# Spread places for routing steps, weights issued in pieces, and part of the softmax sums moved to VectorE in an attention and mixture-of-experts kernel

## The chip, the cores and the metric

The kernel runs on one core of one Trainium2 chip. A core has five engines that run side by side, each with its own in-order queue of instructions: TensorE (PE, matrix products; its weight loads, PEld, overlap them), VectorE (DVE), ScalarE (ACT), GpSimd (POOL) and SyncE (SP, which here only issues DMAs). They meet through semaphores. The metric is the device time of the whole program in microseconds (us).

## The reference

Attention over 8 batches and 12 heads of 448 positions, with a soft cap on the scores, followed by a layer of 8 experts of which each token uses the best one, and each expert keeps at most `capacity` (80) tokens. Cut to what matters:

```python
q, k, v: (8, 12, 448, 64) float32;  cap = 30
scores = cap * tanh((q @ k.T) / 8 / cap)
scores = scores - max(scores)
attn = exp(scores);  attn = attn / (sum(attn) + 1e-9)
x = (attn @ v), heads laid side by side: (3584, 768)

logits = x @ w_gate                         # 8 experts
expert_idx = argmax(logits);  gate_w = softmax(logits)[expert_idx]
out = zeros
for e in range(8):
    tok = tokens of expert e; if more than capacity, those with the largest gate_w
    h = maximum(x[tok] @ w1[e], 0)          # (768, 1024)
    out[tok] = gate_w[tok] * (h @ w2[e])    # (1024, 768)
```

## The kernel before

**Attention.** The 96 pairs of batch and head are worked on in 24 units (`NU`) of four heads. In the loop at L1251, iteration w computes the scores and exps of unit w and, between them, the products with v, the sums and the scaling of unit w-1. The order of the work within an iteration is written out by hand in the list `STEPS` (L1249), and each engine's queue holds its instructions in that order (`manual_schedule`). The steps are:

- `q0` to `q6` (`scores`, L1028): a tile of transposed scores, keys on the partitions, in PSUM (two tiles exist), then ACT's tanh of it. A head's 448 keys are three chunks of 128 and a rest of 64. Tile 0 (L1040) holds the rests of all four heads, two heads' queries stacked on the two halves of the partitions; tiles 1 to 6 (L1049) hold the chunks.
- `e0` to `e3` (`expo`, L1052): ACT's exps, in place, in the unit's tile `e`. Two such tiles exist.
- `p00 p01 p10 p11` (`esum`, L1056): GpSimd adds the three chunks of exps of a pair of heads, in two additions per pair, into a tile `t1`.
- `a00` to `a12` (`av`, L1064) and `r0 r1` (`rests`, L1087): the products of the exps with v for unit w-1, in two PSUM tiles.
- `s`: `total_of` (L1071) sums the exps over the keys with matmuls: four with a matrix of ones over `t1` (L1075), eight with the half masks over the rests in tile 0 (L1078). Then `sums` (L1097): VectorE reads the sums (`st`, L1102) and makes their reciprocals `r`.
- `n0 n1` (`scaled`, L1110): x = av times r on VectorE, which also frees the av tiles for the next iteration's `a00 a10`. After `n1` VectorE transposes x (`turned`, L1116), and for a batch's last unit SP stores it (`xs`, L1125).

**Routing.** Every third unit ends a batch; `gate` (L1135) then queues the logits' product (`lgp`, L1133), its transposes (`lt`, L1147) and the arithmetic (`choice`, `key`, the weights `g` and their store to `gd`, L322). Each batch is ranked against the earlier ones (`ranks`, L376): the keys are laid out as a row (`psk`, L387; `krow`, L388), compared (`gb`, L408; `gl`, L395) and multiplied with ones (`pd`, L415), and VectorE adds the result (`add`, L421). After five batches `prune` (L507) and `order` (L230: o1, o2, three times o3, o4) fix the first experts' order and tokens; the steps after that (`ranked`, `places`, `parts`, `left`, `right`, `kept`, `put`, `keys`, `early`, `rows_in`, `rows_out`) lead to gathers of token rows (L706).

**The planner.** These routing steps are not in `STEPS`. They wait in the lists `urgent`, `low` and `bg`, each with a planned cost in ns on VectorE and a gap in places, and at every `b` of `STEPS`, a place, `background` (L1202) takes some of them. It keeps two clocks: `clock[0]` grows by `PLACE` at each place, and `clock[1]` is the planned end of VectorE's work. The quota of a place is its share of what is queued, at least 600, and the step that overshoots it is still taken. From unit 16 (`LATER`) on, a step is refused when VectorE would then end more than `SLACK` of that place after `clock[0]`.

**Loads.** SP issues all loads of an iteration at its start: q and k of the next unit (`load`, L1003) and v of the present one (`loadv`, L1013), and a part of the zeros of the output (`zfill`). Experts' weights come in 84 chunks (`more`, L730; `wload`, L739), 512 KB of w1 or 384 KB of w2, in expert order; the expert's number is first read into a register from a tile that o4 writes (L252). Seven chunk buffers (`WPRE`) exist during attention, and all seven are issued at the end of iteration 22. Iteration 24 (`LAST`, L1250) holds the products of the last unit and the first expert's first products; then the experts follow.

Of the kernel before, what the change touches and what calls it, by code (L numbers as in the profile page):

```python
# [12 lines left out]
ALU = mybir.AluOpType  # L13
# [4 lines left out]
B, H, S, D = 8, 12, 448, 64  # L18
# [5 lines left out]
KR = S - NK * CK  # L24
# [23 lines left out]
WPRE = 7  # L48
WMORE = 3
AHEAD = 2  # L50
WHOLE = (4, 3)
PLACE = 2450
PLACES = 6
NU = B * NQ
LATER = OB * NQ + 1
SLACK = (9000, 7000, 5000, 3000, 9500, 9500)
LATE = 3
HQ = S // 2
NBUF = 4
# [54 lines left out]
def attn_moe(ctx, tc, q2, k, v, cap, wg, w1, w2, capacity, ct, out):  # L114
    nc = tc.nc
# [18 lines left out]
    ones = consts.tile([128, 128], F32, name="ones")  # L134
# [595 lines left out]
    def more(n):  # L730

        while len(wts) < min(n, len(jobs)):
            k_, v, kk = jobs[len(wts)]
            if v not in regs:
                src = ev0_i if v < NPRE else ev_i
                regs[v] = nc.values_load(src[0:1, v:v + 1], engines=[mybir.EngineType.SP], min_val=0, max_val=E - 1)
            wts.extend(wload(wring, regs[v], f"{v}", [kk if k_ == "a" else KD + kk]))

    def wload(pool, e, tag, chunks=range(KD + KF)):  # L739

        r = []
        for kk in chunks:
            n = F if kk < KD else DM
            w = pool.tile([128, n], F32, name=f"w{tag}_{kk}", tag="w")
            src, i = (w1, kk) if kk < KD else (w2, kk - KD)
            nc.sync.dma_start(w, src[e, :, i, :] if isinstance(e, int) else src[bass.ds(e, 1), :, i, :])
            r.append(w)
        return r
# [239 lines left out]
    def vector(cost):  # L988

        clock[1] = max(clock) + cost  # L990
    st = {"laid": set()}
# [3 lines left out]
    with ExitStack() as a2:  # L995
# [7 lines left out]
        def load(p):  # L1003
            b, j = divmod(p, NP)
            qt = qkp.tile([128, S], F32, name=f"qt{p}", tag="qt", bufs=NBUF)
            kt = qkp.tile([128, S], F32, name=f"kt{p}", tag="kt", bufs=NBUF)
            for h in range(2):
                w = slice(64 * h, 64 * h + 64)
                nc.sync.dma_start(kt[w], k[b, j, :, h])
                nc.sync.dma_start(qt[w], q2[b, j, w, h])  # L1010
            st[p] = dict(q=qt, k=kt)

        def loadv(p):  # L1013
            vr = st[p]["v"] = vp.tile([CK, 2, NK + 1, D], F32, name=f"vr{p}", tag="vr")
            src = v[p // NP, p % NP]
            nc.sync.dma_start(vr[:, :, 0:NK], src[:, :, 0:NK])
            row, head = src.ap[0][0], src.ap[1][0]
            rest = bass.AP(src.tensor, src[:, :, NK].offset, [[row, KR], [KR * row + head, 2], [1, D]])
            for i in range(2):
                nc.sync.dma_start(vr[KR * i:KR * i + KR, :, NK], rest)  # L1020

        def rest_of(u, pr, h):
            return st["e", u][:, h, HQ * pr:HQ * pr + HQ]

        def chunk_of(u, pr, c, h):
            return st["e", u][:, 2 + 2 * NK * pr + 2 * c + h]
# [29 lines left out]
        def esum(u, pr, i):  # L1056
# [4 lines left out]
            else:  # L1061
                nc.gpsimd.tensor_tensor(st["es", u, pr], st["es", u, pr], e[:, 4:6], op=ALU.add)  # L1062

        def av(u, f, c):  # L1064
            if c == 0:
                st["av", u, f] = psa.tile([128, 512], F32, name=f"av{u}_{f}", tag="av", bufs=2)
            for g in range(4):
                nc.tensor.matmul(st["av", u, f][32 * g:32 * g + 32, :S], st[2 * u + g // 2]["v"][:, g % 2, c, 32 * f:32 * f + 32],  # L1068
                                 chunk_of(u, g // 2, c, g % 2), start=(c == 0), stop=(c == NK - 1))

        def total_of(u):  # L1071

            sp = st["sp", u] = ps1.tile([128, 512], F32, name=f"sp{u}", tag="misc", bufs=2)
            for g in range(4):
                nc.tensor.matmul(sp[32 * g:32 * g + 32, :S], ones[:, 0:32], st["es", u, g // 2][:, g % 2], start=True, stop=False)  # L1075
            for i in range(2):
                for g in range(4):
                    nc.tensor.matmul(sp[32 * g:32 * g + 32, HQ * i:HQ * i + HQ], st["half"][:, i], rest_of(u, g // 2, g % 2), start=False, stop=(i == 1))  # L1078

# [7 lines left out]
        def rests(u, part):  # L1087

            for i in range(2):
                f = i ^ part  # L1090
                w = slice(KR * i, KR * i + KR)
                for g in range(4):
                    pr, h = divmod(g, 2)
                    nc.tensor.matmul(st["av", u, f][32 * g:32 * g + 32, HQ * i:HQ * i + HQ], st[2 * u + pr]["v"][w, h, NK, 32 * f:32 * f + 32],  # L1094
                                     rest_of(u, pr, h)[w], start=False, stop=False)
# [105 lines left out]

        def background(quota, took=PLACE, slack=1e9):  # L1202

            now[0] += 1
            clock[0] += took
            for q, last in ((urgent, 1), (low, 3), (bg, 2)):
                while q and quota > 0:  # L1210
                    cost, f, gap = q[0]
                    if gap == "ordered":
                        if not st.get("ordered"):
                            break
                        gap = 1
                    if quota < 1e8:
                        if now[0] < now[last] + gap or (gap and slack < 1e8 and clock[0] < ready_at[last]):
                            break
                        if max(clock) + cost > clock[0] + slack:
                            return  # L1220
                    q.pop(0)
                    quota -= cost
                    vector(cost)
                    now[last] = now[0]
                    ready_at[last] = clock[1]
                    f()
# [19 lines left out]
        load(1)  # L1246
        guards()
        setup()
        STEPS = ("q0 q1 e0 b a00 a10 r0 q2 q3 e1 p00 p01 b a01 a11 b q4 q5 e2 p10 b s r1 a02 q6 e3 p11 n0 a12 n1 b b").split()  # L1249
        LAST = ("b a00 a10 r0 h q b a01 a11 q b s r1 a02 q b a12 q b q b q b").split()  # L1250
        for w in range(NU + 1):  # L1251
            if w == 0:
                manual = ExitStack()
                manual.enter_context(tc.manual_schedule())
            if w + 1 < NU:
                load(2 * w + 2)
                load(2 * w + 3)
            if w < NU:
                loadv(2 * w)
                loadv(2 * w + 1)  # L1260
            if w % NQ == NQ - 1:
                zfill(w // NQ, B)
            todo = STEPS if w < NU else LAST
            turns = list(range(7)) if w else [1, 2, 3, 4, 5, 6, 0]
            runs = ((0, 2), (2, 4), (4, 6), (6, 7)) if w else ((1, 3), (3, 5), (5, 7), (0, 1))
            left = 1 + -w % NQ
            for i, x in enumerate(todo):
                k_ = x[0]
                a_ = [int(y) for y in x[1:]]
                if k_ == 'q' and w < NU:  # L1270
                    scores(w, turns[a_[0]])
                elif k_ == 'q':
                    begin()
                elif k_ == 'e':
                    expo(w, *runs[a_[0]])
                elif k_ == 'p':
                    esum(w, *a_)
                elif k_ == 'a' and w:
                    av(w - 1, *a_)
                elif k_ == 's' and w:  # L1280
                    total_of(w - 1)
                    sums(w - 1)
                elif k_ == 'r' and w:
                    rests(w - 1, a_[0])
                elif k_ == 'h':
                    masks()
                elif k_ == 'n' and 1 <= w < NU:
                    scaled(w - 1, a_[0])
                    if a_[0] == 1:
                        turned(w - 1, 0)  # L1290
                        turned(w - 1, 1)
                        if w % NQ == 0:
                            gate(w // NQ - 1)
                            left = NQ + 1
                elif k_ == 'b' and w:
                    share = sum(c for c, _, _ in bg + urgent) / (PLACES * (left - 1) + todo[i:].count('b'))
                    share += sum(c for c, _, _ in low) / max(1, PLACES * (NU - 1 - w))
                    background(min(max(share, 600), 2200 if w < LATER else 3000), PLACE, SLACK[todo[:i].count('b')] if LATER <= w < NU else 1e9)
            if w == NU - 2:
                more(WPRE)  # L1300

    last_u = B * NQ - 1
    for f in range(2):
# [149 lines left out]
```

## Time and profile before

| | us |
|---|---|
| median of 3 runs | 560.41 (555.8 to 561.76) |
| the profiled execution | 560.26 |
| its span, first to last instruction | 557.8 |
| mean granted TensorE clock | 0.978 of full speed |

The profile shows one execution. For each engine it gives the time it was busy, for each instruction when it ran, and for the idle time before an instruction what ended it, written `[0.70 <-PE sc L1049]`: 0.70 us of waiting, ended by the PE instruction of line 1049 that writes `sc`. Tiles carry the program's names without their numbers. The span in 40 equal slices (13.9 us each), where a digit is the busy share in tenths:

```profile
PE   5799999999999999999969889779299996999893
DVE  1022483456255457644875888555734564147882
ACT  5999789789989878879958778458101111138781
POOL 2466566545545556654515664177610041501000
DMA  5555357667667956847783466355974889989970
```

Attention takes the first 28 slices; the experts, on PE and DMA, the rest.

### The profile page before, as it was taken

What the parts mean: (1) busy time and instruction counts of PE and PEld (TensorE: products, weight loads), DVE (VectorE), ACT (ScalarE), POOL (GpSimd) and SP (SyncE); (2) the same over time, 40 slices, a digit from 0 to 9 for tenths busy, and PEclk for the clock granted to TensorE, in tenths of its full rate; (3) what the DMA queues carried; (4) which work ended last, traced back from release to release, by engine and by line L of the source; (5) the groups of instructions that cost most, each with busy time, mean ns of one, the idle gap of its engine ahead of it and who ended that gap; (6) DMA issues with size and microseconds to landing.
All of it is one profiled execution on the core that took longest, in us unless ns stands there. A gap on an engine that the chain in (4) does not pass through costs nothing.

```text
span 557.8 us, 12745 instructions
## 1 busy us (share of the span) xinstructions
PE 501.6 (90%) x5074; PEld 199.3 (36%) x5074; DVE 295.8 (53%) x760; ACT 371.4 (67%) x359; POOL 239.0 (43%) x166
## 2 busy tenths in 40 slices
PE   5799999999999999999969889779299996999893
PEld 1233333333333333333313223223033443448682
DVE  1022483456255457644875888555734564147882
ACT  5999789789989878879958778458101111138781
POOL 2466566545545556654515664177610041501000
PEclk9999999999999999999989999899799999999998
DMA  5555357667667956847783466355974889989970
GB/s 156 146 147 150 89 124 191 155 171 116 182 163 108 235 123 114 208 102 178 105 219 87 118 103 192 83 143 44 368 258 143 158 236 372 329 270 339 398 251 23
DMA packets 85859, 98.97 MB, mean 177 GB/s; under 512 B 24304, under 2 KB 74384, under 8 KB 85792
## 3 DMA queue, kind: packets, MB, share of 16 engines
q1 hardware_dynamic: 83888, 94.83, 64.2%
q0 software_dynamic: 1440, 3.25, 2.2%
q8 instruction: 42, 0.69, 0.5%
q14 instruction: 25, 0.20, 0.1%
q10 hardware_dynamic: 464, 0.00, 0.0%
HBM read 74.54 MB, written 23.80 MB: 176 GB/s over the span
## 4 chain that ended last, share of the span: by engine, by line
PE 66%; DMA 11%; ACT 9%; DVE 8%; issue 2%; SPq 1%; another core or an unknown queue 1%; POOL 0%; POOLq 0%; DVEq 0%; ACTq 0%
PE av L1068 19%; PE sc L1049 17%; PE hp L765 6%; PE yp L765 5%; DMA w<-in_w_dram 4%; ACT e L1050 4%; PE av L1094 4%; ACT e L1054 4%; DMA gd<-g 3%; PE sp L1075 3%; PE sc L1040 3%; PE sp L1078 3%; DMA vr<-in_v_dram 2%; PE lgp L1133 2%; DMA qt<-in_q_dram 1%
## 5 line engine op out<-in xcount | busy, mean ns | idle before, releaser
L1050 ACT ACTIVATE e<-sc,scl 128x896 f32<-128x896 f32 x168 | 161.1, 1001 | 60.3 <-PE sc L1049 44.2
L1060 POOL TENSOR_TENSOR t<-e 128x896 f32<-128x896 f32 x48 | 100.8, 2101 | 162.1 <-ACT e L1054 157.0
L1054 ACT ACTIVATE e<-e,capt 128x1792 f32<-128x1792 f32 x96 | 153.8, 1602 | 3.1
L1068 PE MATMUL av<-e,vr 128*32 128x448 f32 x1152 | 135.3, 564 | 8.1 <-DVE x L1114 6.2
L1049 PE MATMUL sc<-qt,kt 64*64 64x448 f32 x1152 | 134.4, 560 | 8.5 <-DMA qt<-in_q_dram 4.6
L1062 POOL TENSOR_TENSOR t<-t,e 128x896 f32<-128x896 f32 x48 | 101.5, 2115 | 17.0 <-ACT e L1054 14.5
L1102 DVE STREAM_TRANSPOSE st<-sp 128x448 f32<-128x448 f32 x24 | 15.5, 648 | 92.9 <-PE sp L1078 92.9
L1049 PEld LDWEIGHTS sc<-qt,kt 64*64 64x64 f32 x1152 | 38.0, 134 | 74.4 <-issue 49.8
L408 DVE TENSOR_SCALAR_CACHE_REDUCE gb<-krow,kc 112x896 bf16<-112x896 f32 (+16 forms) x59 | 53.7, 934 | 12.0 <-ACT krow L388 10.1
L1068 PEld LDWEIGHTS av<-e,vr 128*32 128x32 f32 x1152 | 29.7, 111 | 84.7 <-issue 67.0
L765 PE MATMUL hp<-w,xt 128*96 128x512 f32 x96 | 44.7, 600 | 4.9 <-DMA w<-in_w_dram 3.7
L1114 DVE TENSOR_TENSOR x<-av,r 128x448 f32<-128x448 f32 x48 | 29.2, 623 | 16.4 <-PE av L1068 10.2
L823 POOL DMA_INDIRECT out_dram<-ysv,si x6 | 5.7, 949 | 62.7 <-ACT ysv L822 50.8
L765 PE MATMUL yp<-w,thv 128*96 128x384 f32 x96 | 32.5, 489 | 0.0
L1040 PE MATMUL sc<-qt,kt 64*64 64x224 f32 x384 | 26.2, 362 | 4.5 <-ACT e L1050 1.7
L1094 PE MATMUL av<-e,vr 64*32 64x224 f32 x768 | 29.2, 361 | 0.0
L1122 DVE STREAM_TRANSPOSE xb<-x 128x448 f32<-128x448 f32 x48 | 27.9, 619 | 0.0
L755 DVE TENSOR_TENSOR wlb<-w,whb 128x768 fp32r<-128x768 f32 x24 | 21.4, 953 | 7.0 <-ACT whb L753 7.0
L765 PEld LDWEIGHTS hp<-w,xt 128*96 128x96 f32 x96 | 14.4, 163 | 26.8 <-issue 20.1
L1075 PE MATMUL sp<-t,ones 128*32 128x448 f32 x192 | 23.6, 551 | 0.0
L1078 PE MATMUL sp<-e,half 128*32 128x224 f32 x384 | 23.1, 352 | 0.0
L395 DVE SCALAR_TENSOR_TENSOR gl<-krow,kc,ctt 112x112 bf16<-112x112 f32 x32 | 22.0, 687 | 0.0
(237 smaller groups left out, 473.9 us busy)
## 6 DMA issues: line engine op xcount, KB each, us to landing
w<-in_w_dram SPq DMA_DIRECT2D x36, 512.0 KB
w<-in_w_dram SPq DMA_DIRECT2D x48, 384.0 KB
kt<-in_k_dram SPq DMA_DIRECT2D x96, 112.0 KB
qt<-in_q_dram SPq DMA_DIRECT2D x96, 112.0 KB
xs<-xb SPq DMA_DIRECT2D x32, 336.0 KB
vr<-in_v_dram SPq DMA_DIRECT2D x48, 192.0 KB
out_dram<-zero SPq DMA_DIRECT2D x4, 1536.0 KB
out_dram<-zero SPq DMA_DIRECT2D x4, 1152.0 KB
```

The costliest lines, as they stand in the source:

```text
L408: nc.vector.tensor_scalar(g, krow[:, x:y], kp, 0.0, op0=ALU.is_ge, op1=ALU.add, accum_out=a)
L765: nc.tensor.matmul(ps[:, nn, 0:m], a[:, kk, :], bb[:, nn * m:(nn + 1) * m], start=(kk == 0 and i == 0), stop=(kk == last and i == len(pair ...
L1040: nc.tensor.matmul(ps[KR * i:KR * i + KR, h, HQ * pr:HQ * pr + HQ], s["k"][w, y:y + KR], s["q"][w, HQ * i:HQ * i + HQ], start=True, stop=True)
L1049: nc.tensor.matmul(ps[64 * i:64 * i + 64, h, :S], s["k"][w, y:y + 64], s["q"][w], start=True, stop=True)
L1050: nc.scalar.activation(st["e", u][:, 2 * x:2 * x + 2], ps[:, :, :S], AF.Tanh, scale=scl)
L1054: nc.scalar.activation(e, e, AF.Exp, scale=capt)
L1060: nc.gpsimd.tensor_tensor(t1, e[:, 0:2], e[:, 2:4], op=ALU.add)
L1062: nc.gpsimd.tensor_tensor(st["es", u, pr], st["es", u, pr], e[:, 4:6], op=ALU.add)
L1068: nc.tensor.matmul(st["av", u, f][32 * g:32 * g + 32, :S], st[2 * u + g // 2]["v"][:, g % 2, c, 32 * f:32 * f + 32], chunk_of(u, g // 2, c ...
L1075: nc.tensor.matmul(sp[32 * g:32 * g + 32, :S], ones[:, 0:32], st["es", u, g // 2][:, g % 2], start=True, stop=False)
L1078: nc.tensor.matmul(sp[32 * g:32 * g + 32, HQ * i:HQ * i + HQ], st["half"][:, i], rest_of(u, g // 2, g % 2), start=False, stop=(i == 1))
L1094: nc.tensor.matmul(st["av", u, f][32 * g:32 * g + 32, HQ * i:HQ * i + HQ], st[2 * u + pr]["v"][w, h, NK, 32 * f:32 * f + 32], rest_of(u, p ...
```

## The change

Three things change.

1. `SUMS = 15`: in the first 15 units (iterations 1 to 15) the eight half-mask matmuls of `total_of` are left out. A new step `m` has VectorE add the rests' exps into `t1` instead, with four `scalar_tensor_tensor` instructions per unit on 64 partitions x 448 elements, before the sums' matmuls read `t1`. The planner is told 1750 ns for each pair.
2. The six places of a unit move: one now stands after `r0`, one after `a02`; the one after `p01` and one of the two at the end are gone. `PLACE` is 2330 where it was 2450, and four of the six slacks are smaller.
3. The first seven weight chunks are issued two at a time at the ends of iterations 19, 20 and 21, and one at the end of 22.

```diff
-PLACE = 2450
+PLACE = 2330
 PLACES = 6
...
-SLACK = (9000, 7000, 5000, 3000, 9500, 9500)
+SLACK = (9000, 6800, 3500, 1700, 2000, 10000)
+SUMS = 15
...
+        def erest(u, pr):
+            t1 = st["es", u, pr]
+            vector(1750)
+            for i in range(2):
+                w, x = slice(KR * i, KR * i + KR), slice(HQ * i, HQ * i + HQ)
+                e = st["e", u][w, 0:2, HQ * pr:HQ * pr + HQ]
+                nc.vector.scalar_tensor_tensor(t1[w, :, x], t1[w, :, x], 0.0, e, op0=ALU.add, op1=ALU.add)
...
-                nc.tensor.matmul(sp[32 * g:32 * g + 32, :S], ones[:, 0:32], st["es", u, g // 2][:, g % 2], start=True, stop=False)
-            for i in range(2):
+                nc.tensor.matmul(sp[32 * g:32 * g + 32, :S], ones[:, 0:32], st["es", u, g // 2][:, g % 2], start=True, stop=u < SUMS)
+            for i in range(2 if u >= SUMS else 0):
                 for g in range(4):
                     nc.tensor.matmul(sp[32 * g:32 * g + 32, HQ * i:HQ * i + HQ], st["half"][:, i], rest_of(u, g // 2, g % 2), start=False, stop=(i == 1))
...
-        STEPS = ("q0 q1 e0 b a00 a10 r0 q2 q3 e1 p00 p01 b a01 a11 b q4 q5 e2 p10 b s r1 a02 q6 e3 p11 n0 a12 n1 b b").split()
+        STEPS = ("q0 q1 e0 b a00 a10 r0 b q2 q3 e1 p00 p01 m a01 a11 b q4 q5 e2 p10 b s r1 a02 b q6 e3 p11 n0 a12 n1 b").split()
...
+                elif k_ == 'm' and 1 <= w <= SUMS:
+                    erest(w - 1, 0)
+                    erest(w - 1, 1)
...
-            if w == NU - 2:
-                more(WPRE)
+            if w >= NU - 6:
+                more(min(WPRE, 2 * (w - NU + 6)))
```

## The prediction

> **What bounds the kernel now.** The page's first part, then the engines' busy time unit by unit (a window runs from one unit's first score tile, q0, to the next unit's):
>
> ```profile
> PE 501.6 (90%) x5074; PEld 199.3 (36%) x5074; DVE 295.8 (53%) x760; ACT 371.4 (67%) x359; POOL 239.0 (43%) x166
> ...
> 33.44:47.14 13.70, 13.70 (x173) 4.25 (x169) 4.10 (x9) 12.87 (x12) 8.76 (x5) 1.00 0.68 192
> 47.14:63.70 16.56, 15.94 (x188) 5.21 (x184) 5.81 (x12) 14.69 (x14) 11.14 (x6) 1.00 0.24 63
> 63.70:78.86 15.16, 14.40 (x175) 4.71 (x174) 9.25 (x33) 12.43 (x12) 6.69 (x4) 1.00 0.69 171
> 78.86:92.85 13.99, 13.99 (x175) 4.50 (x174) 7.10 (x20) 12.81 (x12) 7.61 (x5) 1.00 0.68 117
> 277.92:298.15 20.23, 15.54 (x188) 4.91 (x185) 13.55 (x36) 12.56 (x11) 8.15 (x5) 0.92 0.59 153
> 314.35:330.70 16.35, 14.40 (x191) 4.81 (x188) 14.51 (x38) 13.51 (x13) 8.48 (x5) 1.00 0.43 60
> 330.70:347.99 17.29, 16.12 (x189) 5.71 (x189) 15.06 (x29) 12.66 (x11) 8.77 (x5) 1.00 0.73 205
> 347.99:372.05 24.06, 20.11 (x201) 7.10 (x197) 13.26 (x34) 14.19 (x16) 9.42 (x7) 0.93 0.50 121
> 372.05:390.75 18.70, 16.92 (x172) 5.43 (x168) 9.27 (x27) 13.05 (x11) 13.98 (x11) 0.91 0.45 50
> 390.75:403.17 12.42, 1.87 (x32) 0.99 (x29) 8.54 (x25) 2.05 (x2) 7.88 (x7) 0.72 1.05 368
> ```
>
> After the colon pair come the length, then PE, PEld, DVE, ACT, POOL busy, granted clock, DMA share, GB/s. The first unit shown, w=2, has PE busy for all of its 13.70 us and ACT for 12.87: PE is the bound, ACT close behind. The units around a gate (w=3, then w=4) leave PE idle for 0.62 and 0.76 us. From w=18 (277.92) on it is another kernel: PE idles 4.69, 1.95, 1.17, 3.95 and 1.78 us in five of the windows, and after the last unit it does 1.87 us of work in 12.42. So there are two things to cost: PE work in the early units, waits in the late ones. The timeline of one early unit:
>
> ```profile
> 42.26 0.96 PE L1075 MATMUL sp<-t,ones 128*32 128x448 f32 x8
> 43.04 0.94 PE L1078 MATMUL sp<-e,half 128*32 128x224 f32 x16
> 43.91 0.61 PE L1094 MATMUL av<-e,vr 64*32 64x224 f32 x16
> 46.38 1.01 ACT L1050 ACTIVATE e<-sc,scl 128x896 f32<-128x896 f32 x1 [0.70 <-PE sc L1049]
> 48.61 2.11 POOL L1062 TENSOR_TENSOR t<-t,e 128x896 f32<-128x896 f32 x1
> 55.84 2.10 POOL L1060 TENSOR_TENSOR t<-e 128x896 f32<-128x896 f32 x1 [5.12 <-ACT e L1054]
> 55.95 0.96 PE L1075 MATMUL sp<-t,ones 128*32 128x448 f32 x8
> ```
>
> The matmuls that the change drops hold PE from 43.04 to 43.91, 0.87 us. ACT waits 0.70 us for tile q6 behind them: that is all the room ACT has in this unit.
>
> **The dropped matmuls (15 units).** In w=1 and w=2 ACT takes over as the bound, so at most its wait of 0.70 goes; I take 0.6 each, 1.2. In the 13 others PE has gate or rank matmuls besides (13.99 against ACT's 12.81 in w=5), and I take the full 0.87: 11.3. Sum 12.5; from below, were ACT the bound everywhere, 15 x 0.6 = 9.
>
> **The gate's steps.** One place now stands between product and turn where two stood together, and one more before the row transposes.
>
> ```profile
> PE lt L1147 <- ACT lgs L1140: 3.1, 5, 0.6
> PE psk L387 <- DVE kc L310: 3.0, 4, 0.8
> ```
>
> The lt transposes go from behind the logits matmul (waiting for ACT's copy) to behind q0 q1 of the next unit; the psk transposes go one place on, behind a01 a11, when kc is long there. Both waits go: 6.1 us. The transposes' own time only moves.
>
> **The four new VectorE adds (step m).** Each is [64 x 448] with two SBUF inputs. The nearest rows, and how such an instruction fares beside GpSimd:
>
> ```profile
> L755 DVE TENSOR_TENSOR wlb<-w,whb 128x768 fp32r<-128x768 f32 x24 | 21.4, 953 | 7.0 <-ACT whb L753 7.0
> L1344 DVE TENSOR_TENSOR xl<-xt,xh 128x192 fp32r<-128x192 f32 x6 | 2.2, 364 | 4.1 <-ACT xh L1343 3.3 <-issue 0.8
> L408 DVE TENSOR_SCALAR_CACHE_REDUCE gb<-krow,kc 112x896 bf16<-112x896 f32 (+16 forms) x59 | 53.7, 934 | 12.0 <-ACT krow L388 10.1 <-PE pd L415 1.9
> ...
> 70.55 0.18 DVE L321 RECIPROCAL g<-g 112x4 f32<-112x4 f32 x1
> 72.41 2.10 POOL L1060 TENSOR_TENSOR t<-e 128x896 f32<-128x896 f32 x1 [8.02 <-ACT e L1054]
> 73.03 1.60 DVE L395 SCALAR_TENSOR_TENSOR gl<-krow,kc,ctt 112x112 bf16<-112x112 f32 x1
> 73.87 0.96 PE L1075 MATMUL sp<-t,ones 128*32 128x448 f32 x8
> 83.06 0.33 DVE L395 SCALAR_TENSOR_TENSOR gl<-krow,kc,ctt 112x112 bf16<-112x112 f32 x1
> ```
>
> 364 ns for 192 elements and 953 for 768 give 626 ns for 448: 2.5 us a unit, 37.6 in 15, on an engine that is half idle. But their place matters. The sum matmul sp now waits for them, and behind sp stand r1, a02, q6 on PE and so ACT. They wait for the last POOL addition of the previous unit, and L395 shows the rest: the same instruction took 0.33 us alone and 1.60 beside a POOL addition, ending when POOL ended (74.63 against 74.51).
>
> In a light unit (w=3, q0 at 47.14): the POOL addition ends at 50.72, 3.6 us in; the adds run until 6.1; POOL starts again 8.7 in and sp comes 8.8 in. 2.7 us spare: hidden, cost nothing. If DVE came 2.7 us later the cover would be gone. In units with rank steps, three places lie between the transposes and m, each one or two steps of about 0.93 (L408): the adds end some 8 us in, still before sp. In the unit after a gate (w=4, q0 at 63.70): the gate's arithmetic ends at 70.73, 7.0 in; the adds run until 9.5; POOL's addition, 8.7 in before and delayed by the 0.47 us of lt that now stand ahead of q2, comes at about 9.2; sp comes 10.17 - 0.76 + 0.47 = 9.9 in. 0.4 us spare, and one add may find POOL ahead of it and come 2.1 late. A rank step L395 may also meet POOL in the new place between sp's reading and n0, and hold back x and the next a00. For the four such units (w=4, 7, 10, 13) the cost lies between 0 and 2.1 each for the add, as much again for the rank step; I take 1.05 each, 4.2.
>
> The Trainium skill (SBUF — State Buffer, Who interferes with whom) says that a DVE instruction with two SBUF inputs contends with a GpSimd instruction that reads SBUF, and that whichever issues first holds the shared ports while the other blocks fully. The trace agrees (1.60 beside, 0.33 alone); by this rule the fourth add, begun before POOL, would make POOL wait and sp would lose nothing.
>
> Early part: 12.5 + 6.1 - 4.2 = 14.4 us gained (ends: 9 + 6.1 - 8.4 = 7, and 19).
>
> **The new slacks (units from w=16).** The unit whose sums end just before 278:
>
> ```profile
> 272.13 2.12 DVE L237 TENSOR_SCALAR okey<-neso 128x8 f32<-128x8 f32 x1 [2.10 <-ACT neso L269]
> 272.56 0.96 PE L1075 MATMUL sp<-t,ones 128*32 128x448 f32 x8
> 281.68 0.64 DVE L1102 STREAM_TRANSPOSE st<-sp 128x448 f32<-128x448 f32 x1
> 284.34 0.98 PE L1068 MATMUL av<-e,vr 128*32 128x448 f32 x4 [4.69 <-DVE x L1114]
> ...
> L252 DVE CAST ev_i<-ev x1: 148/148/148, 286.2 to 286.2; 1x4 int32<-1x4 f32 x1
> ```
>
> DVE reads sp's result 7 us late, because place 3 of w=17 took six steps (o1, two rank steps, o2, two of o3) before it, planned at 550 ns and running up to 2.12 beside POOL. With the costs in the code, a slack of 1700 there lets o1 and the two rank steps in; o2 comes after the read, the rest in the last place. I take 4 of the 4.69. The same happens in w=20 to 22: parts, left, keys leave place 3 for the unit's end. But choice and ranked now fall into the new place between the read and n0, where POOL is busy too. Of the other idle 1.95 + 1.17 + 3.95 + 1.78 = 8.9 us I take 3; ends 8.9 and a loss of 8 (below).
>
> **The weights in pieces.** SP's queue (DMA issues) and PE at the end of attention:
>
> ```profile
> 380.53 0.33 SPq L322 DMA_DIRECT2D gd<-g  x1
> 382.30 9.05 SPq L746 DMA_DIRECT2D w<-in_w_dram  x7
> 391.45 0.59 SPq L1016 DMA_DIRECT2D vr<-in_v_dram  x1
> ...
> 396.02 0.37 PE L415 MATMUL pd<-ones_b,gb 112*128 112x1 bf16 x9 [4.31 <-DVE st L1102]
> 400.71 0.54 PE L415 MATMUL pd<-ones_b,gb 112*128 112x1 bf16 x10 [4.32 <-DVE gb L408]
> 403.17 3.71 PE L1068 MATMUL av<-e,vr 128*32 128x448 f32 x16 [1.92 <-DMA vr<-in_v_dram]
> ```
>
> The last unit's v loads stand behind seven weight issues of 9.05 / 7 = 1.3 us and their 3.6 MB. Now only one is left there: v is issued about 7.8 us sooner and the last 1.9 us of wait go. The two pd waits hang on DVE instead; the DMA queue, full at 368 GB/s, also held up the row gathers that DVE waits for. By the planner's costs one rank product still opens the last round, behind four rank steps and the x transposes: about 5 us of wait where 11.5 were (12.42 less 0.9 of a matmul's rest). I take 5.5 gained; ends 0 and 11.5. The price elsewhere: two pieces stand ahead of the q and k loads issued in w=20, 21, 22: 2.6 us of issue and 1.05 MB, 2.8 us at 368 GB/s. Those loads have a unit's time, so I cost it at nothing; without that cover it is up to 2.6 a unit, 8 in all. The register load that comes first reads ev_i, written at 286.2, well before w=19 ends at 314: SP does not wait. The gd store of that gate falls behind the loads of w=20 in SP's queue, not ahead, which helps. The gathers move on POOL's queue from w=22 to w=23; if they land late, st waits as it did.
>
> **Sum.** The profiled execution took 560.26 us (span 557.8, and 2.5 around it), as good as the median of 560.41. Gains 14.4 + 4 + 3 + 5.5 = 26.9: 533.4.
>
> **Rivals.** *The adds come late.* If in the 12 units with gate or rank steps (w=4 to 15) DVE reaches m later than 6.2 us after q0, the adds meet POOL's pair of additions, one slipping in per addition: sp is two POOL additions late, 4.2 - 0.87 = 3.3 us lost a unit, 40 in all, less 2.1 (w=1 to 3), 6.1 and 12.5: 580. It decides the sign from 1.7 us a unit. For it: L395's 1.60, 0.4 spare in w=4. Against: DVE's 7.10 of 13.99 in w=5. The rule quoted above from the Trainium skill (SBUF — State Buffer, Who interferes with whom) names the same mechanism. *The late part gives nothing.* New waits (loads behind the pieces, choice and ranked before n0) take the 12.5: 560.3 - 14.4 = 546, up to 554 with the 8 us of late loads. For it: DVE busy 14.51 of 16.35 in w=20. Against: the idle of 4.69 has one cause, and it is moved.
>
> **How the numbers follow.** Forecast 0.68, late part gives nothing 0.23, adds late 0.09. The forecast's own range adds the early ends and half of the late ones: 523 to 545. The range that leaves out no more than 2 in 10 reaches over the second case: 523 to 553. A measurement of this kernel can tell about 1% (5.6 us) from no change. Faster takes the first case and nearly all of the second and leaves a little for mishaps: 0.86; same 0.06; slower 0.08.
>
> **What would show it.** L1078 down to 9 units, no lt or psk waits, w=2 near 13.1 us, m's adds near 626 ns and ended before sp, st read on time in w=17, L1016's last issues right behind one weight piece. Wrong: PE waiting at sp for DVE, adds of 2 us, PE waiting for qt or kt from w=20 on.

## The result and the profile after

The changed kernel took 529.43 us (median of 4 runs, 527.48 to 531.19) where the kernel before took 558.35 (median of 4, 555.8 to 561.76): a ratio of 0.948, interval 0.940 to 0.955. Forecast were 533.4 us, 523 to 553. The profiled execution took 527.48 us with a span of 525.6, 32.2 us less than the 557.8 of before. The new code has moved the line numbers: `av` is L1077 now, `sp` L1084 (the half masks L1087), the new additions L1071, `st` L1111, `x` L1123, `gb` L409, `gl` L396. A ratio, here and below, is formed from the executions within 1.5% of the same kernel's fastest, so one of 710.91 us among the four of the kernel with the pieces alone counts in none.

The page's first part, then the engines' busy time unit by unit, columns as before (w=2 to 5, then w=18, 21, 22 and the stretch behind the last unit):

```profile
PE 489.6 (93%) x4834; PEld 191.0 (36%) x4834; DVE 324.1 (62%) x820; ACT 370.4 (70%) x359; POOL 240.6 (46%) x166
```

```profile
32.39:45.33 12.94, 12.94 (x156) 3.72 (x153) 8.91 (x13) 12.81 (x12) 8.78 (x5) 1.00 0.71 200
45.33:59.98 14.65, 14.65 (x168) 4.34 (x165) 10.33 (x16) 14.20 (x13) 10.47 (x6) 1.00 0.27 74
59.98:73.91 13.93, 13.93 (x161) 4.44 (x160) 10.16 (x36) 12.80 (x13) 7.32 (x5) 1.00 0.72 178
73.91:88.86 14.95, 14.13 (x163) 4.47 (x159) 10.68 (x26) 12.92 (x12) 8.27 (x5) 1.00 0.67 115
266.37:281.50 15.13, 15.13 (x206) 5.44 (x202) 10.27 (x30) 13.03 (x12) 8.87 (x5) 1.00 0.77 208
313.62:331.06 17.44, 14.77 (x192) 5.21 (x188) 15.45 (x35) 12.91 (x12) 8.90 (x5) 1.00 0.93 183
331.06:349.74 18.68, 17.34 (x196) 5.99 (x192) 8.67 (x29) 13.65 (x14) 8.29 (x5) 1.00 0.84 201
367.63:373.86 6.23, 1.26 (x20) 0.45 (x16) 5.65 (x15) 2.05 (x2) 5.16 (x5) 0.75 1.11 357
```

Set beside the windows of before: the light unit w=2 went from 13.70 to 12.94, and ACT is now busy for all but 0.13 us of it. The gate's unit w=3 went from 16.56 to 14.65, the unit after it from 15.16 to 13.93, and PE idles in neither. But w=5 grew, from 13.99 to 14.95, although 0.87 us of matmuls left it. In the late part w=18 lost 5.1 us and w=22 5.4, and the stretch behind the last unit is half as long. By stretch, the 32.2 us are these: up to the start of w=16 (249.20 before, 236.46 now) 12.7; from there to the last `av` matmul of w=23 (141.55 long, now 131.17) 10.4; the stretch behind it (12.42, now 6.23) 6.2; and everything after 2.9.

The waits of PE that the prediction named are gone: neither `lt` nor `psk` is in the list any more. What ends PE's idle time now (us in total, times, longest):

```profile
PE pd L416 <- DVE gb L409: 5.0, 1, 5.0
...
PE av L1077 <- DVE x L1123: 3.3, 2, 2.7
```

The place that the forecast was least sure of, the four additions in the unit after a gate (w=4, q0 at 59.98), in the timeline:

```profile
66.92 2.51 DVE L1071 SCALAR_TENSOR_TENSOR t<-t,e 64x448 f32<-64x448 f32 x4
69.16 2.23 POOL L1061 TENSOR_TENSOR t<-e 128x896 f32<-128x896 f32 x1 [6.46 <-ACT e L1055]
69.79 0.96 PE L1084 MATMUL sp<-t,ones 128*32 128x448 f32 x8
73.58 2.17 DVE L396 SCALAR_TENSOR_TENSOR gl<-krow,kc,ctt 112x112 bf16<-112x112 f32 x1
76.35 1.87 PE L1077 MATMUL av<-e,vr 128*32 128x448 f32 x16 [0.59 <-DVE x L1123]
```

The additions end at 69.43 and PE takes up `sp` at 69.79, with no wait: 0.36 us to spare. The last of them, begun at about 68.8 (three times 0.63 us behind the first), was under way when POOL's addition came, and it is POOL's that lasted longer, 2.23 us where 2.10 is usual. The rank step at 73.58 did meet POOL (2.17 us where it takes 0.33 alone) and `x` behind it came 0.59 us late.

The end of attention, SP's queue and PE:

```profile
357.32 0.34 SPq L747 DMA_DIRECT2D w<-in_w_dram  x1
357.77 0.58 SPq L1017 DMA_DIRECT2D vr<-in_v_dram  x1
...
363.65 0.38 DVE L610 STREAM_TRANSPOSE xt<-xge 128x192 f32<-128x192 f32 x1 [5.60 <-DMA xge<-xs,gi]
...
373.56 0.37 PE L416 MATMUL pd<-ones_b,gb 112*128 112x1 bf16 x8 [4.96 <-DVE gb L409]
373.86 3.21 PE L1077 MATMUL av<-e,vr 128*32 128x448 f32 x16
```

The last unit's v now goes out right behind one piece of weights, and one rank product still holds PE for 4.96 us. VectorE, for which it waits, has itself been waiting: the transposes of the gathered token rows (`xt`) stand in its queue ahead of `st` (at 368.31), `x` and the rank step, and they wait 11.1 us for the gathers' DMA in all, as they did before (10.1 us). The 16 matmuls after PE's wait take 3.21 us where they take 1.71 elsewhere.

### The profile page after: what moved, and what is told of

Read it like the earlier page. It is cut to its first block, busy times and chain, and to the rows that moved or that the text cites. A ratio compares the mean times of both kernels' runs of the same rounds, so it can differ in the third digit from the quotient of the medians.

```text
span 525.6 us, 12347 instructions
## 1 busy us (share of the span) xinstructions
PE 489.6 (93%) x4834; PEld 191.0 (36%) x4834; DVE 324.1 (62%) x820; ACT 370.4 (70%) x359; POOL 240.6 (46%) x166
## 4 chain that ended last, share of the span: by engine, by line
PE 73%; DMA 12%; DVE 5%; ACT 4%; SPq 2%; issue 1%; POOL 0%; POOLq 0%; DVEq 0%; ACTq 0%
PE av L1077 19%; PE sc L1050 19%; PE hp L766 11%; PE yp L766 8%; DMA w<-in_w_dram 5%; PE av L1103 4%; PE sp L1084 3%; DMA vr<-in_v_dram 3%; DMA qt<-in_q_dram 3%; PE lgp L1142 2%; PE sc L1041 2%; DMA xge<-xs,gi 2%; PE pd L416 2%; ACT e L1051 2%; ACT e L1055 1%
## 5 line engine op out<-in xcount | busy, mean ns | idle before, releaser
L1077 PE MATMUL av<-e,vr 128*32 128x448 f32 x1152 | 137.6, 557 | 3.9 <-DVE x L1123 3.3
L1063 POOL TENSOR_TENSOR t<-t,e 128x896 f32<-128x896 f32 x48 | 102.5, 2134 | 12.7 <-ACT e L1055 9.5
L1077 PEld LDWEIGHTS av<-e,vr 128*32 128x32 f32 x1152 | 30.1, 110 | 86.6 <-issue 71.4
L1111 DVE STREAM_TRANSPOSE st<-sp 128x448 f32<-128x448 f32 x24 | 15.5, 647 | 73.3 <-PE sp L1087 38.0
L409 DVE TENSOR_SCALAR_CACHE_REDUCE gb<-krow,kc 112x896 bf16<-112x896 f32 (+16 forms) x59 | 53.5, 932 | 6.3 <-PE pd L416 3.0
L1071 DVE SCALAR_TENSOR_TENSOR t<-t,e 64x448 f32<-64x448 f32 x60 | 47.1, 785 | 10.8 <-ACT e L1055 9.9
L1123 DVE TENSOR_TENSOR x<-av,r 128x448 f32<-128x448 f32 x48 | 28.9, 619 | 11.1 <-PE av L1077 9.8
L781 ACT ACTIVATE hsv<-hp 96x1024 f32<-96x1024 f32 x5 | 5.1, 1020 | 29.2 <-PE hp L766 29.2
L1084 PE MATMUL sp<-t,ones 128*32 128x448 f32 x192 | 23.0, 551 | 0.0
```

The source lines that it names most:

```text
L409: nc.vector.tensor_scalar(g, krow[:, x:y], kp, 0.0, op0=ALU.is_ge, op1=ALU.add, accum_out=a)
L1071: nc.vector.scalar_tensor_tensor(t1[w, :, x], t1[w, :, x], 0.0, e, op0=ALU.add, op1=ALU.add)
```

## The experiments

Several chips were used, and the kernel before took 557.0 to 566.4 us on them, so each result is a ratio to the kernel before on the same chip. Starts and lengths of units come from one profiled execution of each kernel and are less sure: w=16 of the changed kernel begins at 236.46 us in one and at 240.11 in another, on another chip.

**One part at a time.** Four kernels, on one chip. First the sums alone: the additions and the dropped matmuls in the kernel before, with its old places.

```diff
-STEPS = ("... e1 p00 p01 b a01 a11 b q4 ...").split()
+STEPS = ("... e1 p00 p01 m b a01 a11 b q4 ...").split()
```

> The kernel before with the VectorE adds of the first 15 units alone; places, planned clock, slacks and weights as before. Theory (PE work is what the early units save, DVE has the room): the 0.87 us of half-mask matmuls goes in 15 units, less what ACT as second bound keeps in the two light ones, and the lt and psk waits (6.1 us) stay: start of unit 16 some 9 to 12.5 us earlier, total 546 to 549. Rival (the adds come late, sp waits for DVE behind POOL's additions): no gain or a loss, 556 to 575, with PE idle before sp.

553.6 us, ratio 0.995 (0.991 to 0.999), between the ranges of the theory and of its rival; w=16 starts only 6.0 us sooner. The light units shrink by 0.76 and the gate units by 0.75, but each of the four units after a gate grows by 0.47, and the `lt` and `psk` waits stay (3.1 and 3.0 us). In w=4 of this kernel:

```profile
67.89 4.34 DVE L1071 SCALAR_TENSOR_TENSOR t<-t,e 64x448 f32<-64x448 f32 x4
69.66 2.09 POOL L1061 TENSOR_TENSOR t<-e 128x896 f32<-128x896 f32 x1 [7.17 <-ACT e L1055]
...
72.38 0.94 PE L1084 MATMUL sp<-t,ones 128*32 128x448 f32 x4 [0.32 <-DVE t L1071]
```

The additions begin 6.93 us after q0 (60.96), in the changed kernel 6.94. What differs is POOL: its addition begins 8.70 us after q0 here and 9.18 there, where `lt` stands between q0 q1 and q2 and no longer ahead of q0. The fourth addition of VectorE, due 0.1 us after POOL's here, meets it, and the four take 4.34 us instead of 2.51. So up to w=16 the sums alone give about half of the 12.5 us that the dropped matmuls were to bring.

Then the places and slacks alone, with the weights in one burst:

```diff
-SUMS = 15
+SUMS = 0
...
-            if w >= NU - 6:
-                more(min(WPRE, 2 * (w - NU + 6)))
+            if w == NU - 2:
+                more(WPRE)
```

> The kernel before with the new places, planned clock and slacks alone; all sums by matmuls, weights in one burst. Theory: lt and psk waits go (6.1 us), the waits of w=18 to 22 shrink by some 7, the rank step that now stands ahead of n0 gives back 1 us in some four units, the last round stays about as it was: 545 to 548. Rival (the places matter only for the adds): 556 to 560.

542.07 us, ratio 0.972 (0.966 to 0.979), more than the theory gave it. Up to w=16 it gains 3.1 us, from w=16 to w=23 another 9.6. Here too the units two behind a gate are longer than before (w=5 14.95, w=8 15.71, before 13.99 and 14.40): whatever lengthens them came with the places and not with the additions.

The pieces alone, in the kernel before:

```diff
-            if w == NU - 2:
-                more(WPRE)
+            if w >= NU - 6:
+                more(min(WPRE, 2 * (w - NU + 6)))
```

> The kernel before with the first seven weight chunks issued in pieces alone. Theory: v of the last unit is issued about 7.8 us sooner, but the two product waits that hang on DVE (4.3 us each) stay unless the gathers speed up: 2 to 6 us, so 552 to 556. Rival A (the burst is the whole cause of the 12 us without products): 546 to 548. Rival B (pieces ahead of the q and k loads delay w=21 to 23 as much): 558 or more.

563.61 us, ratio 1.011 (1.004 to 1.019): about 1% slower, as rival B had it. Two pieces ahead of w=20's loads, and the next unit's first matmuls:

```profile
322.81 0.32 SPq L322 DMA_DIRECT2D gd<-g  x1
324.22 0.96 SPq L746 DMA_DIRECT2D w<-in_w_dram  x2
...
325.85 3.34 SPq L1010 DMA_DIRECT2D qt<-in_q_dram  x1
...
336.40 2.83 PE L1040 MATMUL sc<-qt,kt 64*64 64x224 f32 x10 [4.46 <-DMA qt<-in_q_dram]
```

The issues of q and k behind the pieces stretch over 10.8 us (325.28 to 336.08), and PE stands 4.46 us for q. The prediction had this as the price of its lost cover. What loses the cover here is the gate's store `gd`: SP waits 5.1 us in it for VectorE's `g`, and pieces and loads of w=20 stand behind it. In the changed kernel those loads go out ahead of it:

```profile
302.48 1.19 SPq L1010 DMA_DIRECT2D kt<-in_k_dram  x1
...
314.36 0.56 SPq L323 DMA_DIRECT2D gd<-g  x1
```

And the whole change with the burst in place of the pieces:

```diff
-            if w >= NU - 6:
-                more(min(WPRE, 2 * (w - NU + 6)))
+            if w == NU - 2:
+                more(WPRE)
```

> The changed kernel with the seven chunks issued in one burst at the end of w=22 again. Theory: the last unit's v loads stand behind the burst again, and the row gathers compete with it: 2 to 8 us more than the changed kernel's 529.4, 531 to 537. Rival (the pieces cost at w=21 to 23, by late q and k, what they give at the end): 527 to 530.

534.18 us, ratio 0.958 (0.952 to 0.964): with the new places the pieces are worth about 1%, some 5 us, though the interval still touches that of the changed kernel (0.940 to 0.955). The wait for v that the burst brings is one of 5 us here:

```profile
374.75 0.37 PE L416 MATMUL pd<-ones_b,gb 112*128 112x1 bf16 x8 [8.27 <-DVE gb L409]
380.15 3.97 PE L1077 MATMUL av<-e,vr 128*32 128x448 f32 x16 [5.03 <-DMA vr<-in_v_dram]
```

So the parts do not add up: their ratios alone, 0.995, 0.972 and 1.011, would make 0.978, and the whole has 0.948. In w=4 the sums alone cost 0.47 us and the places alone give 0.47, both together give 1.23; the pieces cost 6.6 us alone and give about 5 with the rest.

**How near the additions are to the edge.** Each addition was followed by one of the same size that changes nothing.

```diff
                 nc.vector.scalar_tensor_tensor(t1[w, :, x], t1[w, :, x], 0.0, e, op0=ALU.add, op1=ALU.add)
+                nc.vector.scalar_tensor_tensor(t1[w, :, x], t1[w, :, x], 0.0, e, op0=ALU.add, op1=ALU.max)
```

> The changed kernel with each add followed by a second instruction of the same size and operands (a maximum that changes nothing): 2.5 us more on DVE in each of the first 15 units. Theory (the adds are hidden as long as they end before sp and before POOL's next addition, with 0.4 us to spare after a gate): units 2 and 3 keep their length, units 4, 7, 10 and 13 become several us longer with PE waiting at sp for DVE, the rank units 1 to 3; total 15 to 35 us more than 529.4, 545 to 565. Rival (DVE has room, its work costs nothing): 529 to 533.

582.05 us, ratio 1.029 (1.022 to 1.036), more than either side expected. The light unit w=2 takes 13.43 us (12.94 without the doubling) and w=3 14.73 (14.65); w=4, 7, 10 and 13 take 23.5 to 24.5. In w=4:

```profile
69.84 2.24 POOL L1061 TENSOR_TENSOR t<-e 128x896 f32<-128x896 f32 x1 [6.71 <-ACT e L1055]
70.17 2.40 DVE L1071 SCALAR_TENSOR_TENSOR t<-t,e 64x448 f32<-64x448 f32 x1
...
72.16 2.34 POOL L1063 TENSOR_TENSOR t<-t,e 128x896 f32<-128x896 f32 x1
72.60 2.39 DVE L1072 SCALAR_TENSOR_TENSOR t<-t,e 64x448 f32<-64x448 f32 x1
...
78.20 1.71 PE L1085 MATMUL sp<-t,ones 128*32 128x448 f32 x4 [6.78 <-DVE t L1072]
```

Once POOL's chain has begun, one addition of DVE gets through per addition of POOL, at 2.40 us each, and PE waits 6.78 us. That is not all: in the window of this unit PE is busy for 16.71 us, where the same work took 13.93 in the changed kernel. The granted clock is why (windows of 3 us, the number before the last two is the clock):

```profile
76.00:79.00 3.00, 0.80 (x4) 0.22 (x4) 2.61 (x6) 0.00 (x0) 0.92 (x1) 0.50 0.74 99
79.00:82.00 3.00, 3.00 (x28) 0.42 (x24) 1.95 (x6) 0.00 (x0) 0.00 (x0) 0.50 0.59 33
```

6.78 of waiting and 2.78 of slow matmuls make the 9.56 us by which w=4 is longer.

**More units with the additions.**

```diff
-SUMS = 15
+SUMS = 23
```

> The changed kernel with the VectorE adds in 23 units instead of 15. Theory: 8 times 0.87 = 7 us of PE work goes, but from unit 16 on DVE has up to 15 us of work in a unit of 17, so most of it is given back in waits at sp and the routing steps slip into the last round: 525 to 532. Rival A (DVE has the room there too): 521 to 523. Rival B (DVE becomes the bound): 534 or more.

543.64 us, ratio 0.961 (0.954 to 0.968), about 1.5% more than the changed kernel, on the side of rival B. From w=16 to w=23 it is shorter (108.9 us, changed 113.3), but with VectorE's time spent there, steps of the routing slip into the last round, where nothing covers them:

```profile
369.99 1.71 PE L566 MATMUL prt<-prrh,prlh 112*96 112x40 bf16 x20 [4.74 <-DVE prrh L560]
```

The same product ran at 328.26 in the changed kernel, among the matmuls of w=21. From the last unit's first `av` matmuls to the end it takes 166.0 us, the changed kernel 151.7.

**The place before n0, the slacks and the last round.** First the new place behind a02 was kept empty in all units:

```diff
-background(..., SLACK[todo[:i].count('b')] if LATER <= w < NU else 1e9)
+background(..., 1e9 if w == NU else -1e9 if idx == 4 else SLACK[idx] if w >= LATER else 1e9)
```

> The changed kernel with the place after a02 kept empty in all units, so that no routing step stands on DVE between the reading of sp and n0. Theory (a rank step held up there by a POOL addition makes x late, and with it a00 of units 5, 8, 11 and 14; ranked does the same to unit 21): these units become 1 us shorter each, unit 21 some 2.5, total 3 to 6 us less than 529.4: 523 to 526. Rival (those units are long for another reason, late v loads or their own product matmuls): 528 to 531.

532.42 us, ratio 0.937 (0.930 to 0.944). That is on the theory's side, but the interval overlaps that of the changed kernel, which had 0.945 (0.940 to 0.950) when run again on another chip, so it settles nothing:

> The changed kernel once more, as the measure for the runs beside it on the same chip: a ratio to the kernel before of 0.94 to 0.955, by every theory.

The next three edits shared the chip with that run. The place behind a02 empty only in w=4, 7, 10 and 13:

```diff
-background(..., SLACK[todo[:i].count('b')] if LATER <= w < NU else 1e9)
+background(..., SLACK[idx] if LATER <= w < NU else -1e9 if idx == 4 and w % NQ == 1 and w < LATER else 1e9)
```

> The changed kernel with the place after a02 kept empty in units 4, 7, 10 and 13 alone. Theory (there a rank step waits for a POOL addition and makes x late for the next unit): units 5, 8, 11 and 14 each 0.5 to 1 us shorter, nothing given back at the gates, 2 to 4 us less than the changed kernel. Rival (closing a place only pushes the steps on, as closing it in all units did at the gates): same within 1 us.

533.41 us, ratio 0.946 (0.941 to 0.950): the same, and w=5, 8, 11, 14 stay at 14.97, 14.36, 14.56 and 14.68 us. So the rank step caught by POOL is not what holds these units. In w=5 `x` is no longer late, but v is:

```profile
76.71 1.70 PE L1077 MATMUL av<-e,vr 128*32 128x448 f32 x12 [0.17 <-DMA vr<-in_v_dram]
78.34 1.14 PE L1103 MATMUL av<-e,vr 64*32 64x224 f32 x16
```

The matmuls of r0, 0.61 us elsewhere, take 1.14: the two causes lie over each other, and taking one away leaves the other.

The old slacks with the new places:

```diff
-SLACK = (9000, 6800, 3500, 1700, 2000, 10000)
+SLACK = (9000, 7000, 5000, 3000, 9500, 9500)
```

> The changed kernel with the six slacks of the kernel before (9000, 7000, 5000, 3000, 9500, 9500) at the new places and the new planned clock. Theory (the slacks of places 2 to 4 keep DVE's steps out of the way of the sums): units 2 to 16 unchanged, units 17 to 23 together 4 to 10 us longer. Rival (where the places stand did it, the slacks add nothing): within 2 us of the changed kernel.

535.99 us, ratio 0.950 (0.946 to 0.955): some 2 us more, with intervals that overlap. In the trace w=20 and 21 are longer (18.29 and 20.64, changed 15.62 and 17.80 on this chip), w=22 shorter (16.81, changed 21.75). The slacks move the waits about; most of the late gain was there without them. The planned clock stayed at 2330 here: with the old 2450 as well, the queues come out in an order in which they wait for each other for ever, so there is no time for it, and places and planned clock are not told apart.

The last round without its first place:

```diff
-        LAST = ("b a00 a10 r0 h q b a01 ...").split()
+        LAST = ("a00 a10 r0 h q b a01 ...").split()
```

> The changed kernel without the first place of the last round, so that no rank product stands ahead of the last unit's av matmuls. Theory (the 5.0 us for which PE waits there for DVE is exposed): start of these matmuls some 5 us sooner, 3 to 5 us less in all. Rival (the wait only moves to the next place, or the tail is bound by the weights' DMA): within 1.5 us of the changed kernel.

535.86 us, ratio 0.947 (0.941 to 0.952): the same. The rank product no longer stands first, and PE waits for `x` in its place. The first line is from the changed kernel on this chip, the second from this run:

```profile
381.66 0.38 PE L416 MATMUL pd<-ones_b,gb 112*128 112x1 bf16 x8 [9.66 <-DVE gb L409]
376.99 3.31 PE L1077 MATMUL av<-e,vr 128*32 128x448 f32 x16 [4.94 <-DVE x L1123]
```

The `av` matmuls do begin 5 us sooner than on this chip's run of the changed kernel (376.99 for 381.96), as the theory had it. But from there to the end this kernel takes 157.0 us and the changed one 151.9, so nothing is gained. 4.1 us of that are PE's busy time, with a granted clock of 0.92 and 0.90 in two stretches of 19.6 us where the changed kernel had 1.00; what brings it down was not followed up.

**What holds the units two behind a gate.** Their loss is found by comparing the duration of one group: the 16 `av` matmuls of step a00 in w=8 take 2.61 us in the changed kernel and took 1.71 before. Timeline of the changed kernel, SP's loads of v in w=7 and that group in w=8 (q0 at 118.19):

```profile
104.26 4.13 SPq L1134 DMA_DIRECT2D xs<-xb  x4
...
117.77 0.56 SPq L1017 DMA_DIRECT2D vr<-in_v_dram  x1
118.38 1.26 SPq L1021 DMA_DIRECT2D vr<-in_v_dram  x2
...
119.86 2.61 PE L1077 MATMUL av<-e,vr 128*32 128x448 f32 x16
```

A load of v lands 2.8 us after its issue (median on the page), so the second one lands at about 120.6, when a00 has been under way for 0.7 us. In the kernel before, that load went out at 122.91, so by the same 2.8 us it landed at 125.7, 0.8 us ahead of a00:

```profile
126.52 1.71 PE L1068 MATMUL av<-e,vr 128*32 128x448 f32 x16
```

Counted from q0 of w=7, SP's queue has hardly moved (that load goes out after 13.7 us, before after 13.5), but a00 comes after 15.8 us where it came after 17.1. The queue from the stores `xs` to the last v takes 15.4 us (104.26 to 119.64), before 16.4 (108.43 to 124.78). The last run puts those stores behind the loads, for all gates but the last:

```diff
             if j == NP - 1:
-                for i in range(4):
-                    nc.sync.dma_start(xs..., st["xt", b][32 * i:32 * i + 32])
+                if b < B - 1:
+                    st["store"] = b
+                else:
+                    stored(b)
...
                 loadv(2 * w + 1)
+            if "store" in st:
+                stored(st.pop("store"))
```

> The changed kernel with one thing moved: the four stores xs<-xb that follow each gate but the last go into SP's queue behind that unit's q, k and v loads, not ahead of them. Nothing else differs. Theory: in the changed kernel the unit after a gate is 1.2 us shorter while SP's queue between the stores and the last v load takes 15.4 us as before, so the v tiles come in after PE has got to a00 of the next unit: there 16 av matmuls take 2.6 to 2.7 us where they took 1.71. With the stores behind, v is issued some 4 us or more sooner: a00 back to 1.71 us in w=8, 11 and 14, these units 13.4 to 13.7 us (14.5 before this edit), w=5 near 14.0 (14.95; its 0.6 us of wait for x stays), w=16 begins at about 232.5 to 234.5 (236.5 to 240.1 in the runs of the changed kernel), and the whole is 3 to 5 us shorter: ratio to the kernel before 0.937 to 0.942 where the changed kernel had 0.945. Rival 1: the v loads are held by something else (the release of their buffers, the bytes on the wire): these units stay within 0.3 us, ratio 0.945. Rival 2: the stores, now late, hold the one buffer xb, so that DVE's turn at the end of the unit after a gate waits for them: up to 2 us in w=4, 7, 10, 13 or in the units behind, which takes the gain back.

Its six times lie between 522.04 and 542.13 us, median 533.53, before 565.87 on this chip. The ratio of 0.930 (0.922 to 0.937) rests on the two shortest alone, and the profile is of the longest. Over all six the median is 0.943 of before, so no better version is shown. In that profile both the theory and its second rival are at work, the first in w=8 here (q0 at 116.67), the second in w=8 and in w=14 (q0 at 205.96):

```profile
118.33 1.71 PE L1077 MATMUL av<-e,vr 128*32 128x448 f32 x16
...
121.23 1.17 DVE L1131 STREAM_TRANSPOSE xb<-x 128x448 f32<-128x448 f32 x2 [3.06 <-DMA xs<-xb]
...
211.58 1.17 DVE L1131 STREAM_TRANSPOSE xb<-x 128x448 f32<-128x448 f32 x2 [4.84 <-DMA xs<-xb]
...
215.05 7.87 DVE L1071 SCALAR_TENSOR_TENSOR t<-t,e 64x448 f32<-64x448 f32 x4
...
218.24 1.65 PE L1084 MATMUL sp<-t,ones 128*32 128x448 f32 x4 [3.00 <-DVE t L1071]
```

With v early, a00 is back to 1.71 us; w=5 takes 14.01 us (14.95) and w=11 13.65 (14.51), both at a granted clock of 1.00. But the stores still read `xb` when VectorE wants to write it; in w=14 that delays VectorE by 4.84 us, the additions begin 9.1 us after q0, meet POOL, take 7.87 us, and the unit lasts 23.97 us instead of 14.61. A second `xb` might give the one without the other; no run shows it. Whether the shorter executions of this kernel escaped the meeting isn't known: only one was profiled.

## Why the prediction was right, and where it wasn't

**The sum.** 26.9 us were forecast for the span, 32.2 came: early 12.7 for 14.4, late 10.4 for 4 + 3, the stretch at the end 6.2 for 5.5, the part behind it 2.9 for nothing. That the early part came so near is partly luck: 4.2 us were set aside there for a loss that did not come, and about as much was lost in another way (below).

**The dropped matmuls and the gate's waits** came as worked out: w=2 shrank by 0.76 (forecast 0.6), w=3 by 1.91 and w=4 by 1.23, where 0.87 and the removed waits, less the moved `lt`, make 1.96 and 1.16. The matmuls themselves were worth 0.76 us a unit and not 0.87, as w=2 shows here and w=2, 8, 11 and 14 with the sums alone: without them 0.89 us pass from `sp` to r1 (69.79 to 70.68), where `sp` alone held PE for 0.78 before (42.26 to 43.04).

**The additions beside POOL.** 0.4 us to spare in w=4, forecast; 0.36 measured. Their median is 621 ns over 60 (forecast 626); those that meet POOL bring the sum to 47.1 us, forecast 37.6. Of the 4.2 us set aside for late additions and rank steps nothing was paid in w=4, 7, 10 and 13. The step that failed is where this term was put: 4.9 us were lost, but in w=5, 8, 11 and 14 (1.83, 1.01, 1.09 and 0.99, if each should have shrunk by 0.87 us of matmuls), mostly by v that came late. In w=5 the rank step that met POOL, which the forecast did name, held `x` for 0.59 us besides; with v early in the last run, 0.60 us of that wait stay. The prediction did not look at SP's queue for v: that it had 0.8 us to spare in w=8 could be read from the trace of before, and the shorter unit uses it up. The last run shows the cause for a00 in w=8 and for w=5 and w=11; in w=14 a00 is back to 1.71 us too, but the unit is longer for another reason.

**The rule from the Trainium skill** (SBUF — State Buffer, Who interferes with whom), that whichever issues first holds the shared ports, was set there against a cost of 1.05 us an addition. The trace agrees with it: the fourth addition, begun first, made POOL's last 2.23 us, and `sp` lost nothing. So the threshold of 6.2 us after q0 for the "adds late" rival was too strict: it is enough that the fourth addition begins before POOL's. 6.94 was in time with POOL at 9.18, and 6.93 was not with POOL at 8.70 (the sums alone).

**The price of that rival** was too low by far. 3.3 us for each missed unit were two POOL additions; with the clock and the further additions let past one by one it is 9.56 with the eight additions of the doubled kernel (w=4), and 9.4 with the plain four in w=14 of the last run. Its mechanism was right, and so was the place where it is nearest.

**The late part.** That `st` would be read on time in w=17 was right, and w=18 gained 5.1 us where 4 were taken. But the slack of 1700 to which this was put down was not needed: VectorE waits 4.59 us for that `sp` in the changed kernel and still 3.32 with the old slacks, and w=18 takes 15.13 and 15.14 us. The new places, with their planned clock, did it; the old slacks lose only about 2 us in all. The 3 us for the other idle time were too few: w=22 alone gave 5.4. Of these 2.6 are idle time of PE (3.95 before, 1.34 now) and 2.8 its busy time (20.11 before, 17.34 now, the granted clock 0.93 before and 1.00 now), for which the sum had no term. `ranked` between the reading of the sums and `x`, which the forecast feared, did come: 2.67 us of wait in w=21, the longest for `x`.

**The pieces.** One piece ahead of the last v was right, as was the remaining wait of 5 (4.96), and "if they land late, st waits as it did" came true for the gathers. An issue of a piece took 0.3 to 1.6 us where 1.3 was forecast for each. The price elsewhere, "up to 2.6 a unit", is covered only with the new places, since there `gd` stands behind the loads: in the old order the whole change of this part is a loss of 1%. One sign named for being wrong did show, PE's wait for q from w=20 on: 0.23 us in w=22 and 1.54 in w=23, against 1.6 us in w=21 before.

**The tail.** 2.9 us of gain behind the last round were not forecast. What went there is PE's wait for the weights' DMA, 3.7 us before and none now. It stays with the old places (3.0 us with the sums alone, 2.9 with the pieces alone) and is 0.7 with the places alone and the burst. So it goes with the places and not with the pieces; by what way they bring the weights sooner stays open.

## What to carry to other kernels

Before a unit of a pipeline is made shorter, read how much time each load of its successor has to spare behind everything ahead of it in its queue; time taken off the bound engine can come back as a load that is late, as 0.8 us to spare did here. An instruction that moves to VectorE with two inputs in SBUF costs what its start against GpSimd's makes of it (0.62 or 2.40 us here), so give it the earliest place, and measure the margin by doubling it. Test the parts of a change both alone and left out: sums, places and pieces here had ratios of 0.995, 0.972 and 1.011 alone and 0.948 together.

## What the runs showed of the hardware

A long wait of PE costs more than its length. After the 4.96 us of wait in the last round and after the 6.78 us with doubled additions, the granted clock was 0.50 for about 4 us, and after the first 16 `av` matmuls took 3.21 us instead of 1.71; after the 2.67 us of w=21 they took 1.71. The Trainium skill (TensorE: Matmul & The Clock Gate, Part 1: The HAM clock gate) says that the clock halves after about 3.4 us of idleness and comes back after about 3.4 us of work; these three waits agree. Two shorter waits do not: after 3.00 us in w=14 of the last run and after 3.03 us in w=21 of the kernel with doubled additions the clock was 0.50 as well, so here some 3 us were enough.

When both queues are full, these additions of VectorE and GpSimd alternate, one instruction each, and one of VectorE's then seems to last as long as one of GpSimd's (2.40 us for an addition that takes 0.62 alone, beside 2.24 to 2.45 us for GpSimd's).
